# A routed feed-forward kernel: the transposes of the next pass's rows take their place on VectorE behind the last result issued before them

## The chip, the cores and the metric

The kernel runs on one core of one Trainium2 chip. The metric is the device time of one execution in microseconds (us), and the median over several executions. The engines are named as the profile names them: PE (matrix products; PEld is its loading of weights), DVE (VectorE), ACT (ScalarE), POOL (GpSimd) and SP (SyncE, which here issues loads). PE writes its results to PSUM, from which DVE and ACT read them.

## The reference

`x` is (8, 3584, 192), float32. What is computed, in short:

```python
w   = softmax(weight)                             # 8 heads x 7 taps
y   = causal 7-tap convolution of x along the sequence, one set of taps for each 24 channels
y   = y.reshape(28672, 192)                       # tokens
lg  = y @ w_gate + modality_bias[modality_id]     # 8 experts
e   = argmax(lg);  g = softmax(lg)[e]             # one expert and one gate for each token
out = g * (relu(y @ w1[e]) @ w2[e])               # 192 -> 1024 -> 192
```

## The kernel before

**Two halves that overlap.** The tokens are convolved and gated on PE and the other engines in 19 groups. Each finished row is written, with its gate and its number, to a table in DRAM called `routed_rows`, sorted by expert; POOL does this with indirect DMAs (L212). The second half reads that table back. It is cut into *slots*: a slot is a run of rows of one expert, of 1 to 4 *passes* of T = 256 rows each (`PASSES_OF_SLOT`). The first and the last slots are short; the last ones, planned for what is left of each expert, are one pass long. The first half is done long before the last slots, which then run alone.

**A pass.** Products of float32 values are made of a rounded high part and the rest: `sxh`, `sxl`, `sxs` for the rows (`sxs` holds both parts of the last 64 channels), `w1b` and `w2b` for the weights, `hh` and `hl` for the hidden layer. A pass has four steps of 256 hidden units. In a step `first` puts ten products for 128 x 512 values into a PSUM buffer `hps` (L700); ACT makes `hh` of it (relu and rounding, L703), DVE makes `hl` (the rest, L704). `second` multiplies `hh` and `hl` by `w2b` into two buffers `po` (L718, L722); it runs `LAG` = 2 steps behind `first`, so the last two seconds of a pass stand among the first steps of the next one. After the fourth `second` comes `put`, for each of the two `po`: ACT scales one half by the gate (`lowp`, L734), DVE adds the other (`o`, L736), and POOL writes the 128 rows of `o` to their places in the output (L737). There are two `hps` and two `po` buffers, so PE can begin the next pass's `po` only when `o` has been read out of the old one.

**Rows and weights for the next pass.** SP loads the rows of two passes at a time (a *lot*) as `near` (128 channels), `far` (64 channels) and `tags` (gate and row number), L650; there are three buffers of `near` and of `far`. `Slot.turn(k)` brings the rows of one pass into the shape that PE wants: DVE transposes in squares of 32 (`tp<-near` L676, `tp<-far` L678, two `tp` buffers), ACT rounds (`sxh`, `sxs`, L685), DVE subtracts (`sxl`, `sxs`, L687). The program issues the turn of the next pass in the second step (`fp == TURN`, L873) of the current one. Weights of the next slot are split by the same pair, ACT L100 and DVE L101, into eight parts spread over the steps of a slot: in a slot of one pass all eight fall into that pass, in a slot of four passes two into each. Groups of the first half also use L100 and L101, for `xh`/`xl` among others.

**Order.** ACT keeps the order in which the program is written (`ORDERED`, L898). The order on the other engines is chosen by a scheduler, which may move an instruction ahead of others when their data dependences allow it. `tc.issue_after(ins)` makes what is issued under it keep behind `ins` on its queue. `hl` and `o` are the DVE results of a pass; the two transposes depend only on the loads of `near` and `far` and on a free `tp`.

Of the kernel before, what the change touches and what calls it, by code (L numbers as in the profile page):

```python
# [14 lines left out]
ALU = mybir.AluOpType  # L15
# [17 lines left out]
T = 256  # L33
# [10 lines left out]
def conv_then_routed_ffn(ctx, tc, x, weight, modality, w_gate, mod_bias, w1, w2, out):  # L44
    nc = tc.nc
    NB, S, D = x.shape
# [9 lines left out]
    NJ = T // P  # L56
    OVER = 2
    Q = 32
# [25 lines left out]
    def ring(pool, n, shape, dtype, name, tag=None):  # L84

        tag = tag or name
        k = turns[tag] = turns.get(tag, -1) + 1
        return pool.tile(shape, dtype, name=name, tag=f"{tag}_{k % n}", bufs=1)

    def f(ap):  # L90
        return ap.bitcast(F32)
# [19 lines left out]
    def warm(n):  # L111
# [9 lines left out]
        out=tri, in_=ones, compare_op=ALU.is_gt, fill=0.0, base=0,  # L121
# [102 lines left out]
    class Group:  # L224
# [71 lines left out]
        def turn(self, q):  # L296

            t0 = 4 * q % NB
            self.turned = ring(gp, 2, [P, NK, 4, Q], F32, "turned")
            nc.vector.transpose(out=self.turned.rearrange("p k t c -> p t k c"),  # L300
                                in_=self.ys[4 * q // NB][:, t0:t0 + 4, OVER:W].rearrange("p t (k c) -> p t k c", c=Q))
# [32 lines left out]
        def choose(self):  # L334

            n = self.tiles
            lg = self.lg

            def per_tile(ap):
                return ap.unsqueeze(2).broadcast_to([MB, n, E])  # L340

            top = rt.tile([MB, NT], F32, name="top")[:, 0:n]
            nc.vector.tensor_reduce(out=top, in_=lg, axis=AX.X, op=ALU.max)
            ex = rt.tile([MB, NT, E], F32, name="ex", bufs=1)[:, 0:n]
            nc.vector.tensor_tensor(out=ex, in0=lg, in1=per_tile(top), op=ALU.subtract)
            nc.scalar.activation(out=ex, in_=ex, func=AF.Exp)
            self.oh = rt.tile([MB, NT, E], BF16, name="oh")[:, 0:n]
            rk = rt.tile([MB, NT, E], F32, name="rk", bufs=1)[:, 0:n]
            nc.vector.tensor_tensor(out=rk, in0=lg, in1=per_tile(top), op=ALU.is_equal)
            nc.vector.tensor_tensor(out=rk, in0=rk, in1=ramp.unsqueeze(1).broadcast_to([MB, n, E]), op=ALU.mult)  # L350
            first = rt.tile([MB, NT], F32, name="first")[:, 0:n]
            nc.vector.tensor_reduce(out=first, in_=rk, axis=AX.X, op=ALU.max)
            nc.vector.tensor_tensor(out=self.oh, in0=rk, in1=per_tile(first), op=ALU.is_equal)
            den = rt.tile([MB, NT], F32, name="den")[:, 0:n]
            nc.vector.tensor_reduce(out=den, in_=ex, axis=AX.X, op=ALU.add)
            nc.vector.tensor_scalar(out=den, in0=den, scalar1=1e-9, scalar2=None, op0=ALU.add)
            for i, y in enumerate(self.ys):
                nc.vector.reciprocal(out=y[0:MB, 0:self.nb, 0], in_=den[:, i * self.nb:(i + 1) * self.nb])
                with tc.issue_after(state["scatter"]) if "scatter" in state else nullcontext():
                    nc.gpsimd.iota(y.bitcast(I32)[0:MB, 0:self.nb, 1], pattern=[[S, self.nb]],  # L360
                                   base=self.b0 * S + (self.block + i) * MB + MB - 1,
                                   channel_multiplier=-1)
# [118 lines left out]
    state, tables = {}, {}  # L481
# [123 lines left out]
            routed(chunk, ins)  # L605


    class Slot:


# [62 lines left out]
        def turn(self, k):  # L673
            lot, k0 = divmod(k, LOT)
            tp = ring(sp, 2, [P, NJ + 1, P], F32, "tp")
            nc.vector.transpose(out=tp[:, 0:NJ].rearrange("p j (s t) -> p (j s) t", t=Q),  # L676
                                in_=self.rows[lot][:, k0 * T // Q:(k0 + 1) * T // Q])
            nc.vector.transpose(out=tp[:, NJ].rearrange("p (s t) -> p s t", t=Q), in_=self.ends[lot][:, k0])  # L678
            xh = ring(sp, 2, [P, NJ, P], F32R, "sxh")
            xl = ring(sp, 2, [P, NJ, P], F32R, "sxl")  # L680
            xs = ring(sp, 2, [P, NJ, P], F32R, "sxs")
            pieces = [(xh, xl, tp[:, 0:NJ, :])]
            pieces += [(xs[halves[j], j, :], xs[halves[1 - j], j, :], tp[halves[j], NJ, :]) for j in range(NJ)]
            for hi, _, raw in pieces:
                nc.scalar.copy(out=hi, in_=raw)  # L685
            for hi, lo, raw in pieces:
                turned = nc.vector.tensor_tensor(out=lo, in0=raw, in1=f(hi), op=ALU.subtract).ins  # L687
            self.h["x", k] = [z.rearrange("p j s -> p (j s)") for z in (xh, xl, xs)]
            self.h["tag", k] = self.tags[lot][:, k0 * NJ:(k0 + 1) * NJ]
            state["vector"] = turned  # L690

        def first(self, k, fp):
            wa = w1b[self.i % 2]
            mv = self.h["x", k]
            hps = ring(ps_g1, 2, [P, 2, T], F32, "hps")
            for u in range(2):
                fs = slice((2 * fp + u) * P, (2 * fp + u + 1) * P)
                terms = ((0, 0), (0, 1), (2, 0), (1, 2), (3, 2))
                for n, (c, z) in enumerate(terms):
                    nc.tensor.matmul(hps[:, u, :], wa[:, c, fs], mv[z], start=n == 0, stop=n == len(terms) - 1)  # L700
            hh = ring(hp, 3, [P, 2, T], F32R, "hh")
            hl = ring(hp, 3, [P, 2, T], F32R, "hl")
            nc.scalar.activation(out=hh, in_=hps, func=AF.Relu)  # L703
            nc.vector.scalar_tensor_tensor(out=hl, in0=hps, scalar=0.0, in1=f(hh), op0=ALU.max, op1=ALU.subtract)  # L704
            self.h[k, fp] = hh, hl

        def second(self, k, fp):
# [22 lines left out]
        def put(self, tag):  # L730
            for j, po in enumerate(self.po):
                gate = tag[:, j, 0:1]
                lowp = ring(sp, 2, [P, D], F32, "lowp")
                nc.scalar.activation(out=lowp, in_=po[:, D:2 * D], func=AF.Copy, scale=gate)  # L734
                o = ring(sp, OUTS, [P, D], F32, "o")
                nc.vector.scalar_tensor_tensor(out=o, in0=po[:, 0:D], scalar=gate, in1=lowp, op0=ALU.mult, op1=ALU.add)  # L736
                st = nc.gpsimd.indirect_dma_start(  # L737
                    out=out, out_offset=bass.IndirectOffsetOnAxis(ap=tag.bitcast(I32)[:, j, 1:2], axis=0),
                    in_=o, in_offset=None, bounds_check=N - 1, oob_is_err=False).ins
                tc.declare_no_dep(st, group="out", reason="each row is written once")  # L740
                tc.add_to_no_dep_group("out", st)
# [156 lines left out]
    with tc.manual_schedule(engines=ORDERED):  # L898
        run(0, always)
    state.pop("load")  # L900
    n_live = nc.values_load(state["n_live"][0:1, 0:1], min_val=0, max_val=plan[-1][1])
    with tc.If(n_live > always - plan[-1][0]):
        start(always)
# [26 lines left out]
```

## Time and profile before

| what | value |
|---|---|
| median of 3 runs | 1307.16 us (1306.64 to 1310.5) |
| profiled execution | 1303.86 us, its span 1302.1 us |
| PE busy | 1230.6 us (95%) |
| PEld busy | 1196.0 us (92%) |
| DVE busy | 1005.1 us (77%) |
| ACT busy | 725.3 us (56%) |
| POOL busy | 525.9 us (40%) |
| mean granted PE clock | 0.976 |
| HBM read / written | 118.16 / 51.82 MB |

The profiled execution is one of its own, beside the three timed ones. Times in a row count from the start of its span. A row of the timeline gives the start and the duration of one instruction, its engine, line, operation and tiles (output <- inputs), and in brackets how long the engine had waited and for what. A row of a window gives the busy time and the count of each engine in that stretch. `SPq` is the queue of DMA issues on SP. PE stands at nine tenths or more in all slices of the span but the first few and the last three.

### The profile page before, as it was taken

To read this page: it belongs to the slowest core of one execution; us is meant where nothing else is said; L and a number is where in the kernel's file an instruction comes from. 1 tells how busy PE (TensorE), PEld (TensorE's weight loads), DVE (VectorE), ACT (ScalarE), POOL (GpSimd) and SP (SyncE) were. 2 spreads that over 40 slices of the span, in tenths; PEclk is the share of its full clock that TensorE was granted. 3 is DMA by queue.
4 is the path that set the end of the run, shared out by engine and by line. 5 is a ranking of instruction groups with operands and counts; after the bars stand their busy time and mean duration, and the time that the engine had idled before them with its cause. 6 is when DMAs were issued, how large, how long until landed. Compare 5 with 4: busy or idle time off the path is not lost.

```text
span 1302.1 us, 28498 instructions
## 1 busy us (share of the span) xinstructions
PE 1230.6 (95%) x9106; PEld 1196.0 (92%) x9106; DVE 1005.1 (77%) x2545; ACT 725.3 (56%) x1644; POOL 525.9 (40%) x574
## 2 busy tenths in 40 slices
PE   8659998999999999999999999999999999999877
PEld 7438898999999999999999999999999999989877
DVE  6559986787888788887888788877886666677774
ACT  2226564556565656656665556565555555556663
POOL 5744763535353432625353532625344222221221
PEclk9769998999999999999999999999999999999998
DMA  6567474335444445423446345523533234883130
GB/s 176 156 182 155 142 177 89 94 82 138 101 113 98 103 94 118 130 58 98 86 117 150 98 90 122 135 53 92 103 82 90 43 96 97 177 198 100 28 92 16
DMA packets 314837, 142.24 MB, mean 109 GB/s; under 512 B 229043, under 2 KB 301356, under 8 KB 314677
## 3 DMA queue, kind: packets, MB, share of 16 engines
q1 hardware_dynamic: 289060, 94.97, 34.3%
q0 software_dynamic: 23232, 44.30, 10.8%
q8 instruction: 73, 1.20, 0.4%
q10 hardware_dynamic: 2384, 1.06, 0.3%
q14 instruction: 88, 0.71, 0.2%
HBM read 118.16 MB, written 51.82 MB: 131 GB/s over the span
## 4 chain that ended last, share of the span: by engine, by line
PE 73%; DVE 8%; DMA 7%; issue 4%; POOL 3%; SPq 3%; ACT 1%; DVEq 0%; POOLq 0%
PE hps L700 33%; PE po L718 22%; PE po L722 10%; PE cv L276 5%; PE gt L320 3%; POOL routed_rows L212 2%; DMA out_dram<-o,tags 2%; SPq L650 2%; DMA raw<-in_moe_w_dram 2%; DVE hl L704 1%; DVE w1b L101 1%; DMA near<-routed_rows 1%; DVE w2b L101 1%; DVE turned L300 1%; POOL out_dram L737 1%
## 5 line engine op out<-in xcount | busy, mean ns | idle before, releaser
L718 PE MATMUL po<-w2b,hh 128*128 128x384 f32 x1824 | 560.1, 357 | 22.8 <-DVE o L736 22.5
L703 ACT ACTIVATE hh<-hps 128x512 fp32r<-128x512 f32 x456 | 273.2, 599 | 409.9 <-PE hps L700 404.8
L700 PE MATMUL hps<-sxh,w1b 128*128 128x256 f32 x1824 | 486.6, 289 | 3.4 <-DVE hl L704 3.3
L737 POOL DMA_INDIRECT out_dram<-o,tags x228 | 240.1, 1053 | 575.7 <-DVE o L736 510.9
L722 PE MATMUL po<-w2b,hl 128*128 128x192 f32 x1824 | 443.8, 253 | 0.0
L704 DVE SCALAR_TENSOR_TENSOR hl<-hps,hh 128x512 fp32r<-128x512 f32 x456 | 310.9, 682 | 161.1 <-ACT hh L703 157.2
L718 PEld LDWEIGHTS po<-w2b,hh 128*128 128x128 f32 x1824 | 345.4, 189 | 27.5 <-DVE o L736 27.1
L700 PE MATMUL hps<-sxs,w1b 128*128 128x256 f32 x1824 | 365.6, 282 | 0.8 <-DVE sxs L687 0.8
L700 PEld LDWEIGHTS hps<-sxh,w1b 128*128 128x128 f32 x1824 | 346.4, 190 | 11.0 <-DVE hl L704 6.4
L722 PEld LDWEIGHTS po<-w2b,hl 128*128 128x128 f32 x1824 | 347.4, 191 | 0.0
L212 POOL DMA_INDIRECT routed_rows<-y,idx x256 | 253.7, 991 | 150.6 <-issue 102.5
L700 PEld LDWEIGHTS hps<-sxs,w1b 128*128 128x128 f32 x1824 | 281.8, 190 | 1.3 <-DVE sxs L687 1.0
L700 PE MATMUL hps<-sxl,w1b 128*128 128x256 f32 x912 | 257.2, 282 | 0.6 <-DVE sxl L687 0.6
L700 PEld LDWEIGHTS hps<-sxl,w1b 128*128 128x128 f32 x912 | 173.8, 191 | 3.0 <-DVE sxl L687 0.8
L101 DVE TENSOR_TENSOR w1b<-raw,w1b 128x512 fp32r<-128x512 f32 x152 | 102.4, 684 | 10.3 <-ACT w1b L100 8.7
L734 ACT ACTIVATE lowp<-po,tags 128x192 f32<-128x192 f32 x228 | 83.7, 418 | 32.2 <-PE po L718 31.7
L281 ACT COPY y<-cv 112x192 f32<-112x192 f32 (+1 forms) x198 | 53.7, 319 | 82.5 <-PE cv L276 58.0
L736 DVE SCALAR_TENSOR_TENSOR o<-po,tags,lowp 128x192 f32<-128x192 f32 x228 | 84.8, 410 | 16.3 <-DMA out_dram<-o,tags 13.1
L101 DVE TENSOR_TENSOR w2b<-raw,w2b 128x384 fp32r<-128x384 f32 x152 | 82.4, 552 | 15.1 <-ACT w2b L100 15.1
L100 ACT CAST w1b<-raw 128x512 fp32r<-128x512 f32 x152 | 92.3, 621 | 0.7
L100 ACT CAST w2b<-raw 128x384 fp32r<-128x384 f32 x152 | 76.0, 513 | 1.0
L687 DVE TENSOR_TENSOR sxs<-tp,sxs 64x128 fp32r<-64x128 f32 x228 | 66.3, 291 | 7.4 <-ACT sxs L685 0.4
(133 smaller groups left out, 1037.7 us busy)
## 6 DMA issues: line engine op xcount, KB each, us to landing
raw<-in_moe_w_dram SPq DMA_DIRECT2D x38, 768.0 KB
raw<-in_moe_w_dram SPq DMA_DIRECT2D x38, 512.0 KB
raw<-in_moe_w_dram SPq DMA_DIRECT2D x76, 256.0 KB
xr<-in_x_dram SPq DMA_DIRECT2D x36, 384.0 KB
near<-routed_rows SPq DMA_DIRECT2D x212, 64.0 KB
x<-in_x_dram SPq DMA_DIRECT2D x26, 384.0 KB
far<-routed_rows SPq DMA_DIRECT2D x456, 16.0 KB
routed_rows<-filler SPq DMA_DIRECT2D x8, 776.0 KB
```

The lines of the kernel that those rows point to most:

```text
L100: nc.scalar.copy(out=hi, in_=raw)
L101: return nc.vector.tensor_tensor(out=lo, in0=raw, in1=f(hi), op=ALU.subtract).ins
L212: state["scatter"] = nc.gpsimd.indirect_dma_start(out=scr, out_offset=bass.IndirectOffsetOnAxis(ap=idx, axis=0), in_=src, in_offset=None,).ins
L687: turned = nc.vector.tensor_tensor(out=lo, in0=raw, in1=f(hi), op=ALU.subtract).ins
L700: nc.tensor.matmul(hps[:, u, :], wa[:, c, fs], mv[z], start=n == 0, stop=n == len(terms) - 1)
L703: nc.scalar.activation(out=hh, in_=hps, func=AF.Relu)
L704: nc.vector.scalar_tensor_tensor(out=hl, in0=hps, scalar=0.0, in1=f(hh), op0=ALU.max, op1=ALU.subtract)
L718: nc.tensor.matmul(po, hh[:, u, js], wb[:, c, :], start=c == 0, stop=c == NF - 1, skip_group_check=True)
L722: nc.tensor.matmul(po[:, 0:D], hl[:, u, js], wb[:, c, 0:D], start=False, stop=False, skip_group_check=True)
L734: nc.scalar.activation(out=lowp, in_=po[:, D:2 * D], func=AF.Copy, scale=gate)
L736: nc.vector.scalar_tensor_tensor(out=o, in0=po[:, 0:D], scalar=gate, in1=lowp, op0=ALU.mult, op1=ALU.add)
L737: st = nc.gpsimd.indirect_dma_start(out=out, out_offset=bass.IndirectOffsetOnAxis(ap=tag.bitcast(I32)[:, j, 1:2], axis=0), in_=o, in_offse ...
```

## The change

A function `turn_behind` keeps the last instruction made by `hl` or `o`, and `turn` issues its two transposes behind the one that is kept. Nothing else is changed; lines behind it move by 3 to 4.

```diff
+    def turn_behind(op):
+        state["o"] = op.ins
...
         def turn(self, k):
             lot, k0 = divmod(k, LOT)
             tp = ring(sp, 2, [P, NJ + 1, P], F32, "tp")
-            nc.vector.transpose(out=tp[:, 0:NJ].rearrange("p j (s t) -> p (j s) t", t=Q),
-                                in_=self.rows[lot][:, k0 * T // Q:(k0 + 1) * T // Q])
-            nc.vector.transpose(out=tp[:, NJ].rearrange("p (s t) -> p s t", t=Q), in_=self.ends[lot][:, k0])
+            with tc.issue_after(state["o"]) if "o" in state else nullcontext():
+                nc.vector.transpose(out=tp[:, 0:NJ].rearrange("p j (s t) -> p (j s) t", t=Q),
+                                    in_=self.rows[lot][:, k0 * T // Q:(k0 + 1) * T // Q])
+                nc.vector.transpose(out=tp[:, NJ].rearrange("p (s t) -> p s t", t=Q), in_=self.ends[lot][:, k0])
...
-            nc.vector.scalar_tensor_tensor(out=hl, in0=hps, scalar=0.0, in1=f(hh), op0=ALU.max, op1=ALU.subtract)
+            turn_behind(nc.vector.scalar_tensor_tensor(out=hl, in0=hps, scalar=0.0, in1=f(hh), op0=ALU.max, op1=ALU.subtract))
...
-                nc.vector.scalar_tensor_tensor(out=o, in0=po[:, 0:D], scalar=gate, in1=lowp, op0=ALU.mult, op1=ALU.add)
+                turn_behind(nc.vector.scalar_tensor_tensor(out=o, in0=po[:, 0:D], scalar=gate, in1=lowp, op0=ALU.mult, op1=ALU.add))
...
     with tc.manual_schedule(engines=ORDERED):
         run(0, always)
     state.pop("load")
+    state.pop("o")
```

The queue of DVE, in the last slots of one pass each, before the change. `raw_1_86` and `raw_1_88` are the next slot's weights as loaded, `w1b_90` and `w2b_764` the places of their low parts; x2 is two of the same in a row.

```order
L704 SCALAR_TENSOR_TENSOR hl<-hps,hh 128x512
L676 STREAM_TRANSPOSE tp<-near 128x256
L736 SCALAR_TENSOR_TENSOR o<-po,tags,lowp 128x192 x2
L101 TENSOR_TENSOR w1b_90<-raw_1_86,w1b_90 128x512 x2
L687 TENSOR_TENSOR sxl<-tp,sxh 128x256
L687 TENSOR_TENSOR sxs<-tp,sxs 64x128 x2
L704 SCALAR_TENSOR_TENSOR hl<-hps,hh 128x512
L101 TENSOR_TENSOR w2b_764<-raw_1_88,w2b_764 128x2x192 x2
L678 STREAM_TRANSPOSE tp<-far 128x128
L704 SCALAR_TENSOR_TENSOR hl<-hps,hh 128x512
```

Here the transpose of `near` stands ahead of the two `o`, and it belongs to a later pass than the `sxl` and `sxs` behind them. The same place with the change:

```order
L708 SCALAR_TENSOR_TENSOR hl<-hps,hh 128x512
L740 SCALAR_TENSOR_TENSOR o<-po,tags,lowp 128x192 x2
L680 STREAM_TRANSPOSE tp<-near 128x256
L101 TENSOR_TENSOR w1b_90<-raw_1_86,w1b_90 128x512 x2
L682 STREAM_TRANSPOSE tp<-far 128x128
L691 TENSOR_TENSOR sxl<-tp,sxh 128x256
L691 TENSOR_TENSOR sxs<-tp,sxs 64x128 x2
L708 SCALAR_TENSOR_TENSOR hl<-hps,hh 128x512
L101 TENSOR_TENSOR w2b_764<-raw_1_88,w2b_764 128x2x192 x2
L708 SCALAR_TENSOR_TENSOR hl<-hps,hh 128x512
```

Both transposes now stand behind the two `o`, and those of a pass directly ahead of its own `sxl` and `sxs`, with two weight splits between them.

The queue of DVE in a pass in the middle of the run that also splits a part of `x` for the first half (the pass that runs from 786 us in the trace), before the change:

```order
L704 SCALAR_TENSOR_TENSOR hl<-hps,hh 128x512
L736 SCALAR_TENSOR_TENSOR o<-po,tags,lowp 128x192 x2
L101 TENSOR_TENSOR xl<-xr,xh 128x768
L101 TENSOR_TENSOR w1b_90<-raw_1_86,w1b_90 128x512
L687 TENSOR_TENSOR sxl<-tp,sxh 128x256
L687 TENSOR_TENSOR sxs<-tp,sxs 64x128 x2
L704 SCALAR_TENSOR_TENSOR hl<-hps,hh 128x512
L101 TENSOR_TENSOR xl<-xr,xh 128x768
L676 STREAM_TRANSPOSE tp<-near 128x256
L704 SCALAR_TENSOR_TENSOR hl<-hps,hh 128x512
```

The transposes of this pass's turn are not among these rows: they had been issued earlier, and the one in the ninth row belongs to the next turn. With the change:

```order
L708 SCALAR_TENSOR_TENSOR hl<-hps,hh 128x512
L740 SCALAR_TENSOR_TENSOR o<-po,tags,lowp 128x192 x2
L680 STREAM_TRANSPOSE tp<-near 128x256
L682 STREAM_TRANSPOSE tp<-far 128x128
L101 TENSOR_TENSOR xl<-xr,xh 128x768
L101 TENSOR_TENSOR w1b_90<-raw_1_86,w1b_90 128x512
L691 TENSOR_TENSOR sxl<-tp,sxh 128x256
L691 TENSOR_TENSOR sxs<-tp,sxs 64x128 x2
L708 SCALAR_TENSOR_TENSOR hl<-hps,hh 128x512
L101 TENSOR_TENSOR xl<-xr,xh 128x768
```

Both transposes now follow the two `o`, ahead of the splits of `x` and of the weights. On ACT and POOL the order is the same as before, on PE one pair of instructions is swapped, and on SP a few loads of `xr` (L254) stand among the loads of `near` at two places.

## The prediction

> **What bounds the kernel now.** I read the busy time by stage first. Each row gives a stretch, its length, then busy time and count for PE, PEld, DVE, ACT and POOL, and the granted PE clock.
>
> ```profile
> 990.00:1146.00 156.00, 156.00 (x1209) 156.00 (x1209) 106.76 (x255) 84.28 (x188) 33.69 (x34) 1.00 0.49 104
> 1146.00:1281.00 135.00, 119.31 (x871) 117.50 (x871) 101.86 (x227) 83.03 (x185) 27.34 (x24) 0.96 0.39 92
> ```
>
> Until 1146 us PE is never idle, so nothing that DVE does there can gain much. From 1146 us on PE stands still 15.7 of 135 us. To size that stretch I count passes: each pass issues two `lowp`, and these rows count them (DVE, then ACT), and then come the first matmuls of three passes.
>
> ```profile
> 988.30:1146.40 158.10, 12.62 (x34) 12.48 (x34) 1.00 0.49 104
> 1146.40:1280.70 134.30, 8.64 (x24) 8.80 (x24) 0.96 0.39 92
> ...
> 988.37 0.30 PE L700 MATMUL hps<-sxh,w1b 128*128 128x256 f32 x1
> 1146.49 0.31 PE L700 MATMUL hps<-sxh,w1b 128*128 128x256 f32 x1
> 1280.81 0.30 PE L700 MATMUL hps<-sxh,w1b 128*128 128x256 f32 x1
> ```
>
> So 17 passes took 158.12 us, 9.30 each, with PE full; the next 12 took 134.32 us where 12 × 9.30 is 111.6. These last passes cost 22.7 us more than PE needs. The waits of that stretch (1146 to 1281 us), in us, times and longest, say why:
>
> ```profile
> PE po L718 <- DVE o L736: 12.6, 6, 4.1
> PE hps L700 <- DVE hl L704: 3.1, 1, 3.1
> DVE tp L676 <- DMA near<-routed_rows: 16.1, 7, 4.3
> ```
>
> PE's 15.7 us fall together with DVE's 16.1 us. One of the six cases in order of time, DVE, ACT, PE and the SP queue:
>
> ```profile
> 1202.60 0.69 DVE L704 SCALAR_TENSOR_TENSOR hl<-hps,hh 128x512 fp32r<-128x512 f32 x1 [0.42 <-ACT hh L703]
> 1205.56 0.45 DVE L676 STREAM_TRANSPOSE tp<-near 128x256 f32<-128x256 f32 x1 [2.27 <-DMA near<-routed_rows]
> 1205.93 0.70 DVE L736 SCALAR_TENSOR_TENSOR o<-po,tags,lowp 128x192 f32<-128x192 f32 x2
> 1206.55 1.28 DVE L101 TENSOR_TENSOR w1b<-raw,w1b 128x512 fp32r<-128x512 f32 x2
> ...
> 1202.83 0.73 ACT L734 ACTIVATE lowp<-po,tags 128x192 f32<-128x192 f32 x2 [0.26 <-PE po L718]
> ...
> 1206.36 0.44 PE L718 MATMUL po<-w2b,hh 128*128 128x384 f32 x1 [2.12 <-DVE o L736]
> ...
> 1200.34 1.86 SPq L650 DMA_DIRECT2D near<-routed_rows  x4
> ```
>
> The inputs of `o` were ready when `lowp` ended at 1203.56, but `o` started only after the transpose ahead of it, which waited for rows asked for at 1200.34. `o` frees the PSUM bank that PE's next `po` needs, so PE stood 2.12 us for a transpose whose result nobody wanted for another pass.
>
> **The gain at the end.** With the change the transpose ahead of these `o` is gone; the one behind them reads rows that landed about a pass earlier. The row asked for at 1200.34 had landed by 1205.56. In the new order its reader comes after the next pass's `o`. A pass starts at 1198.26 (row below) and its `o` would end at 1203.29 + 0.74 = 1204.03, 5.8 us in; the next starts some 9.7 us later (worked out below), so its `o` end near 1213.7, 8 us after the landing. All 15.7 us of waits go. The remaining 7.0 of the 22.7 us are mostly PE at a low clock behind the gaps:
>
> ```profile
> 1162.00:1166.00 4.00, 4.00 (x21) 4.00 (x22) 2.04 (x4) 1.00 (x3) 0.00 (x0) 0.61 0.37 94
> 1230.00:1234.00 4.00, 4.00 (x21) 4.00 (x20) 3.70 (x9) 1.14 (x3) 1.65 (x2) 0.58 0.14 49
> 1266.00:1270.00 4.00, 3.58 (x18) 3.56 (x19) 3.90 (x11) 0.00 (x0) 2.46 (x2) 0.69 0.14 35
> ...
> 1228.96 0.44 PE L718 MATMUL po<-w2b,hh 128*128 128x384 f32 x1 [2.06 <-DVE o L736]
> ```
>
> At clocks of 0.61, 0.58 and 0.69 these stretches lose 0.39, 0.42 and 0.31 of 4 us, 4.5 us together, behind gaps of 3.1, 2.06 and 4.1 us. Without the gaps I let them go. The Trainium skill, "TensorE: Matmul & The Clock Gate", Part 1 on the clock gate, says that the array falls to half clock only after an idle window of about 3.4 us; by that the first two spells would not come from these gaps and 3.2 us would stay, and the sum below would be 3.2 us higher. The trace disagrees, with a spell right behind 2.06 us.
>
> **What the move costs at the end.** Moving behind `o` puts both transposes between `o` and the splits of the next pass's squares. ACT has a fixed order: `lowp`, weight casts, casts of `sxh` and `sxs` (which need the transposes), then `hh`; DVE's `hl` needs that `hh`, and the next pass's first matmul writes the PSUM buffer that this `hl` reads.
>
> ```profile
> 1210.37 0.30 DVE L678 STREAM_TRANSPOSE tp<-far 128x128 f32<-128x128 f32 x1
> ...
> 1204.79 0.62 ACT L685 CAST sxs<-tp 64x128 fp32r<-64x128 f32 x2
> 1205.43 0.60 ACT L703 ACTIVATE hh<-hps 128x512 fp32r<-128x512 f32 x1
> ...
> 1198.26 0.30 PE L700 MATMUL hps<-sxh,w1b 128*128 128x256 f32 x1
> ```
>
> In the new order (`hl`, `o` twice, near, `w1b` twice, far, splits), with those durations and 0.08 us of overlap between neighbours as in the rows: `o` end 1204.03; near 1203.95 to 1204.40; two `w1b` to 1205.60; far to 1205.82; ACT's two `sxs` casts wait for it, to 1206.5; `hh` to 1207.1; `hl` to 1207.8. Without any stall the next pass would start at 1198.26 + 9.30 = 1207.56. So it starts 0.3 to 0.45 us late; I take 0.4 for each of the seven passes with doubled weight splits: 2.8 us. The bounds are 0 (the far transpose hidden, as in a pass whose `hl` is in time) and 1.0 each (both transposes and a `w1b` split in full). Gain at the end: 22.7 − 2.8 = 19.9 us.
>
> **What it costs before 1146 us.** A plain pass, in which the transposes stood behind the third `hl`:
>
> ```profile
> 1012.00 0.74 DVE L736 SCALAR_TENSOR_TENSOR o<-po,tags,lowp 128x192 f32<-128x192 f32 x2
> 1012.72 0.57 DVE L101 TENSOR_TENSOR w2b<-raw,w2b 128x384 fp32r<-128x384 f32 x1
> 1014.33 0.69 DVE L704 SCALAR_TENSOR_TENSOR hl<-hps,hh 128x512 fp32r<-128x512 f32 x1
> 1014.94 0.44 DVE L676 STREAM_TRANSPOSE tp<-near 128x256 f32<-128x256 f32 x1
> 1015.30 0.27 DVE L678 STREAM_TRANSPOSE tp<-far 128x128 f32<-128x128 f32 x1
> ...
> 1012.88 0.62 ACT L685 CAST sxs<-tp 64x128 fp32r<-64x128 f32 x2
> 1013.53 0.60 ACT L703 ACTIVATE hh<-hps 128x512 fp32r<-128x512 f32 x1
> ...
> 1016.24 0.31 PE L700 MATMUL hps<-sxh,w1b 128*128 128x256 f32 x1
> ```
>
> `hl` ends 1015.02, 1.2 us before it is needed. After the change: near to 1013.1, `w2b` to 1013.6, far to 1013.8, `sxs` casts to 1014.4 (0.9 later), `hh` to 1015.05, `hl` to 1015.8. That uses 0.75 of the 1.2 us; nothing reaches PE. That room is the cover: were the chain 0.5 us longer than I make it, every further tenth would cost a tenth in each such pass. Passes that also split `x` or the gate's squares have no room left:
>
> ```profile
> 791.24 0.74 DVE L736 SCALAR_TENSOR_TENSOR o<-po,tags,lowp 128x192 f32<-128x192 f32 x2
> 792.27 0.96 DVE L101 TENSOR_TENSOR xl<-xr,xh 128x768 fp32r<-128x768 f32 x1 [0.29 <-ACT xh L100]
> 794.84 0.69 DVE L704 SCALAR_TENSOR_TENSOR hl<-hps,hh 128x512 fp32r<-128x512 f32 x1
> ...
> 795.58 0.38 PE L700 MATMUL hps<-sxh,w1b 128*128 128x256 f32 x1
> ...
> 928.81 0.69 DVE L704 SCALAR_TENSOR_TENSOR hl<-hps,hh 128x512 fp32r<-128x512 f32 x1
> 929.55 0.39 PE L700 MATMUL hps<-sxh,w1b 128*128 128x256 f32 x1
> ```
>
> Here the next pass starts 0.05 us after `hl` ends. The transposes (0.36 and 0.27 us from start to start) come ahead of `xl`, which idled 0.29 us anyway; near to 792.34 and far to 792.5 make `xl` some 0.2 us late, and `hl` and PE with it. Sixteen passes between 190 and 930 us end so, the last at 929.55: 16 × 0.2 = 3.2 us, between 0 (the idle time hides all) and 16 × 0.63 = 10 us (it hides nothing).
>
> The wait attached by the change names an instruction of DVE's own queue and adds no semaphore. The casts, splits and `hh` stay where they are on ACT. On SP a few loads of `xr` now stand among the `near` loads of a lot at two places, and would hold them until `xl` has read the buffer, some 8 us later than their turn. SP then waits far longer for DVE's slot table before its next weights, so this costs nothing; without that cover it would be one late weight load, about 6 us each.
>
> ```profile
> SPq L615 <- DVE of L562: 37.5, 2, 18.8
> ```
>
> **Sum.** The profiled execution took 1303.86 us (span 1302.1, 1.8 around it): 1303.86 − 19.9 + 3.2 = 1287.2. It was 3.3 us quicker than the median of the runs, 1307.16, and below the lowest of them, 1306.64. The same 16.7 us off the median give **1290.5 us**.
>
> **The rivals.** *The room is smaller than I make it.* In its favour: the plain pass keeps less than 0.5 us, and the chain crosses between DVE and ACT three times. Against: the rows show 0.03 us from `sxs` to `hh`. If some 90 passes each lost 0.1 us, the time would be 1290.5 + 9 = 1299.5. *Slower:* the same cover gone altogether. ACT's `hh` behind casts that wait for the transposes makes `hl` late at every pass start. It decides from the point where the chain is 0.7 us longer than computed, since 90 passes then lose 0.22 us each, the 19.9 us of the end; at 0.25 us over the forecast it would be 1290.5 + 22.5 = 1313. No idle time in DVE's rows of a plain pass speaks for that. *The rows are still late:* the transposes, now behind `o`, hold `hl` instead. With half of the 12.6 us left it would be 1297. Against it stand the 8 us of lead; for it, that SP asks for these rows only after weight splits which the change itself delays by tenths. *Nothing comes of it,* because the waits move to another instruction of the same queue: 1307. The new order of DVE speaks against that.
>
> **Numbers.** The forecast has 0.66, the smaller room 0.15, late rows 0.08, no effect 0.06, slower 0.05. About 0.3% (3.9 us) is what a measurement of this kernel can tell from none. Faster: 0.66 + 0.08 + 0.12 of the 0.15 = 0.86; the same 0.03 + 0.06 = 0.09; slower 0.05. The range: downwards the forecast without any cost at the end and before (1284.5), and a little for the jitter of the runs, 1283; upwards the smaller room, 1301.
>
> **What would show it.** Right: after 1146 us no `tp` waits for `near`, no `po` of PE waits for `o`, twelve passes take about 114.4 us instead of 134.3, and the clock stays at 1.00 there. Each end pass shows PE waiting 0.3 to 0.45 us for `hl`. Before 1146 us passes such as the one at 786 us take 0.2 us more, and plain ones stay at 9.30. Wrong: plain passes longer than 9.30, ACT's `sxs` waiting for `tp` by over 1.5 us, or `tp` waiting for `near` behind `o`.

## The result: 31.5 us faster, about twice what was forecast

| | before | with the change |
|---|---|---|
| median | 1306.9 us (1304.99 to 1310.5, 4 runs) | 1275.36 us (1274.14 to 1276.73, 4 runs) |
| profiled execution | 1303.86 us, span 1302.1 | 1274.14 us, span 1272.4 |

The ratio is 0.9756, with a 95% interval from 0.9732 to 0.9779. The forecast was 1290.5 us, with a range from 1283 to 1301: the direction was right, the size was not, and 1275.36 lies below the range.

The 29.7 us between the two profiled executions can be laid out by the starts of passes (the first `hps` product of each in the timelines). I number passes by when they start in the trace of before.

| stretch | before | with the change | difference |
|---|---|---|---|
| to the start of the pass at 190 us | 190.36 | 189.56 | -0.8 |
| from there to the pass at 1146 us | 956.13 | 946.46 | -9.7 |
| the next twelve passes | 134.32 | 114.59 | -19.7 |
| the rest of the span | 21.29 | 21.79 | +0.5 |

The prediction had -19.9 for the third row and +3.2 for the second. So the end went as forecast, and the middle, where a small loss was forecast, gained.

**The end.** The stretches before and in the last twelve passes of the changed kernel (length, then busy time and count of PE, PEld, DVE, ACT, POOL, the granted PE clock, DMA share, GB/s), and then the first products of the first of these passes and of the one after the last:

```profile
978.00:1136.00 158.00, 158.00 (x1225) 158.00 (x1225) 106.55 (x262) 88.26 (x190) 35.39 (x36) 1.00 0.50 105
1136.00:1251.00 115.00, 113.92 (x869) 112.10 (x868) 101.02 (x226) 83.25 (x184) 25.08 (x24) 1.00 0.46 106
...
1136.02 0.31 PE L704 MATMUL hps<-sxh,w1b 128*128 128x256 f32 x1
1250.61 0.39 PE L704 MATMUL hps<-sxh,w1b 128*128 128x256 f32 x1
```

PE now stands still 1.1 of 115 us where it stood 15.7 of 135, and the clock is 1.00 throughout where it was 0.96. The waits of that stretch (us, times, longest) no longer hold a `tp` that waits for `near`, nor a `po` that waits for `o`:

```profile
ACT sxs L689 <- DVE tp L682: 8.0, 12, 1.0
PEld hps L704 <- DVE hl L708: 2.7, 7, 0.6
PE hps L704 <- DVE hl L708: 0.3, 1, 0.3
```

One of the last passes (it starts at 1192.42), DVE and then ACT, to be held against the case shown in the prediction:

```profile
1197.56 0.74 DVE L740 SCALAR_TENSOR_TENSOR o<-po,tags,lowp 128x192 f32<-128x192 f32 x2
1198.22 0.43 DVE L680 STREAM_TRANSPOSE tp<-near 128x256 f32<-128x256 f32 x1
1198.58 1.25 DVE L101 TENSOR_TENSOR w1b<-raw,w1b 128x512 fp32r<-128x512 f32 x2
1199.75 0.30 DVE L682 STREAM_TRANSPOSE tp<-far 128x128 f32<-128x128 f32 x1
1201.36 0.69 DVE L708 SCALAR_TENSOR_TENSOR hl<-hps,hh 128x512 fp32r<-128x512 f32 x1 [0.33 <-ACT hh L707]
...
1200.09 0.62 ACT L689 CAST sxs<-tp 64x128 fp32r<-64x128 f32 x2 [0.91 <-DVE tp L682]
```

`o` runs at once, the near transpose behind it finds its rows there, and the far one behind the two weight splits makes ACT's `sxs` casts 0.91 us late, so that `hl` ends 9.63 us into the pass. The seven last passes take 9.68 us each.

**The middle.** The stretch that the prediction passed over, in the kernel before and then (nearly the same passes) in the changed one:

```profile
190.00:990.00 800.00, 791.07 (x6007) 783.30 (x6006) 648.88 (x1597) 468.39 (x1049) 349.53 (x375) 1.00 0.44 103
```

```profile
189.00:980.00 791.00, 789.12 (x6012) 781.98 (x6012) 647.48 (x1596) 476.20 (x1049) 343.66 (x373) 1.00 0.44 104
```

Before, PE stood still 8.9 us in these 800 us; now 1.9 in 791. DVE's waits over the whole span, before and then with the change, name what has gone:

```profile
DVE tp L676 <- DMA near<-routed_rows: 18.1, 8, 4.3
DVE o L736 <- DMA out_dram<-o,tags: 13.1, 8, 4.4
```

```profile
DVE o L740 <- DMA out_dram<-o,tags: 1.8, 3, 0.9
```

`o` has four buffers, and a new `o` has to wait until the store of the fourth last has read its own. Four passes carry the whole gain:

| pass that starts (before) at | before | with the change |
|---|---|---|
| 190 us | 18.06 | 10.98 |
| 325 us | 12.49 | 10.74 |
| 390 us | 12.26 | 10.74 |
| 682 us | 11.83 | 10.74 |

That is 11.4 us. Against it stand the losses that were forecast: of the sixteen passes that the prediction counted (they end right after an `hl`), three are the ones at 325, 390 and 682 us; the other thirteen became 0.05 to 0.25 us longer, 1.8 us in all.

The size of these stalls differs between executions with one and the same order. In the profiles of e1 and e6 below, which keep the old order there, the pass at 190 us takes 18.64 and 16.25 us, and the one at 682 us 11.30 and 10.76.

How a transpose comes to hold a store can be followed in the trace of before. Here are DVE, POOL, and at the end DVE and PE again; L374 to L387 is the placement, in which a group of the first half works out to which rows its tokens go (`idx`):

```profile
168.64 0.45 DVE L676 STREAM_TRANSPOSE tp<-near 128x256 f32<-128x256 f32 x1 [2.00 <-DMA near<-routed_rows]
169.01 0.24 DVE L374 COPY ad<-rp 112x120 f32<-112x120 f32 x1
171.98 0.17 DVE L387 CAST idx<-row 112x16 int32<-112x16 f32 x1
...
172.94 0.95 POOL L212 DMA_INDIRECT routed_rows<-y,idx  x1 [7.61 <-ACT y L281]
193.87 1.64 POOL L737 DMA_INDIRECT out_dram<-o,tags  x1 [0.15 <-DVE hl L704]
...
200.65 0.42 DVE L736 SCALAR_TENSOR_TENSOR o<-po,tags,lowp 128x192 f32<-128x192 f32 x1 [4.45 <-DMA out_dram<-o,tags]
...
201.12 0.69 PE L718 MATMUL po<-w2b,hh 128*128 128x384 f32 x1 [4.77 <-DVE o L736]
```

The same places with the change:

```profile
166.15 0.28 DVE L374 COPY ad<-rp 112x120 f32<-112x120 f32 x1
168.33 0.18 DVE L387 CAST idx<-row 112x16 int32<-112x16 f32 x1
...
169.31 0.95 POOL L212 DMA_INDIRECT routed_rows<-y,idx  x1 [4.38 <-issue]
189.82 1.03 POOL L741 DMA_INDIRECT out_dram<-o,tags  x1 [0.15 <-issue]
...
195.05 0.80 DVE L740 SCALAR_TENSOR_TENSOR o<-po,tags,lowp 128x192 f32<-128x192 f32 x2
```

The transpose of rows that are wanted two passes later waits 2.0 us, and the placement stands behind it on DVE, most of it behind the transpose of `far` as well. `idx` is 3.6 us later than it is with the change (3.2 us by the start of its pass). POOL's first scatter (L212) starts 0.8 us after it in both kernels; sixteen scatters take 21 us; only then come the stores of `o`. The store that starts at 193.87 has not landed when `o` wants its buffer. Before, `idx` ended 3.62 us after the start of its pass, and now 0.39; for the placements ahead of the other three stalls it ends 0.93, 0.53 and 0.52 us earlier than before, by the starts of passes.

### The profile page after: what moved, and what is told of

The parts are those of the page before. It is cut to its first block, busy times and chain, and to the rows that moved or that the text cites. A ratio compares the mean times of both kernels' runs of the same rounds, so it can differ in the third digit from the quotient of the medians.

```text
span 1272.4 us, 28546 instructions
## 1 busy us (share of the span) xinstructions
PE 1221.3 (96%) x9106; PEld 1187.7 (93%) x9106; DVE 1001.7 (79%) x2545; ACT 736.9 (58%) x1644; POOL 519.2 (41%) x574
## 4 chain that ended last, share of the span: by engine, by line
PE 77%; DVE 7%; issue 4%; DMA 4%; POOL 3%; SPq 2%; ACT 2%; DVEq 0%; POOLq 0%; ACTq 0%
PE hps L704 36%; PE po L722 23%; PE po L726 11%; PE cv L276 5%; PE gt L320 3%; POOL routed_rows L212 2%; DVE hl L708 2%; SPq L653 2%; DVE w1b L101 1%; DMA raw<-in_moe_w_dram 1%; DMA routed_rows<-y,idx 1%; DVE w2b L101 1%; DMA near<-routed_rows 1%; ACT lowp L738 0%; DVE sxs L691 0%
## 5 line engine op out<-in xcount | busy, mean ns | idle before, releaser
L741 POOL DMA_INDIRECT out_dram<-o,tags x228 | 233.6, 1024 | 555.8 <-DVE o L740 492.2
L704 PEld LDWEIGHTS hps<-sxh,w1b 128*128 128x128 f32 x1824 | 343.9, 189 | 12.7 <-DVE hl L708 7.9
L212 POOL DMA_INDIRECT routed_rows<-y,idx x256 | 253.7, 991 | 145.4 <-issue 114.2
L101 DVE TENSOR_TENSOR w2b<-raw,w2b 128x384 fp32r<-128x384 f32 x152 | 80.9, 542 | 10.3 <-ACT w2b L100 10.0
L689 ACT CAST sxs<-tp 64x128 fp32r<-64x128 f32 x228 | 67.9, 298 | 32.6 <-DVE tp L682 29.8
```

The costliest lines, as they stand in the source:

```text
L101: return nc.vector.tensor_tensor(out=lo, in0=raw, in1=f(hi), op=ALU.subtract).ins
L212: state["scatter"] = nc.gpsimd.indirect_dma_start(out=scr, out_offset=bass.IndirectOffsetOnAxis(ap=idx, axis=0), in_=src, in_offset=None,).ins
L741: st = nc.gpsimd.indirect_dma_start(out=out, out_offset=bass.IndirectOffsetOnAxis(ap=tag.bitcast(I32)[:, j, 1:2], axis=0), in_=o, in_offse ...
```

## The experiments

Each was timed against the kernel before on the same chip. The gain is worked out from the ratio and its interval and from the median of before in that call (1303 to 1304 us, 1306.9 for the change itself). The profile of each is cut in two as above: "early" from the second pass to the pass at 1146 us, "end" the next twelve passes. The start of the second pass moved between 99.5 and 104.9 us over all the profiles, whatever the kernel, so the stretches tell more than spans do. Chunk 8 holds the slots of two passes near the end, chunk 9 the last slots of one pass.

| run | gain in us (95%) | early | pass at 190 us | end |
|---|---|---|---|---|
| before | - | 1045.2 | 18.06 | 134.3 |
| the change | 31.9 (28.9 to 35.0) | 1036.3 | 10.98 | 114.6 |
| e1_end_only | 17.6 (15.4 to 19.7) | 1045.5 | 18.64 | 114.4 |
| e2_early_only | 10.3 (6.8 to 13.7) | 1036.8 | 11.30 | 133.7 |
| e3_one_turn | 2.7 (0.8 to 4.7) | 1042.3 | 15.72 | 133.0 |
| e4_before_o7 | 11.2 (9.0 to 13.4) | 1032.2 | 11.18 | 133.8 |
| e5_near_only | 21.1 (18.5 to 23.6) | 1041.7 | 15.79 | 117.4 |
| e6_rows_ready | 16.3 (13.2 to 19.3) | 1042.2 | 16.25 | 117.2 |
| e7_turn2 | -4.2 (-6.1 to -2.3) | 1060.1 | 11.99 | 121.3 |
| e8_after_o7 | 32.2 (29.6 to 34.8) | 1035.3 | 10.81 | 114.4 |
| e9_after_again | 29.1 (26.1 to 32.1) | 1037.3 | 11.35 | 114.6 |
| e10_two_slots | 7.0 (4.0 to 10.0) | 1038.5 | 11.01 | 134.9 |
| e11_far_free | 25.6 (22.3 to 28.7) | 1035.4 | 11.48 | 117.0 |
| e12_far_free_o7 | 28.8 (25.7 to 31.9) | 1033.3 | 10.80 | 114.2 |

### Two gains, or one

The condition at `turn` is narrowed to the end (e1) or to all but the end (e2):

```diff
-            with tc.issue_after(state["o"]) if "o" in state else nullcontext():
+            with tc.issue_after(state["o"]) if "o" in state and self.chunk >= 8 else nullcontext():
```

> Transposes go behind the last result only in the slots of two passes and of one pass at the end (chunks 8 and 9); everywhere else the scheduler places them as before. Theory (two separate gains): the twelve passes from about 1146 us take 114.6 us as in the changed kernel instead of 134.3, and the passes before stay as in the kernel before, the one of 18.06 us at 190 us among them: about 1287 us, 19 to 20 us under before. Rival (one gain, the earlier passes became quicker because of something that the end shares): over 1290 or under 1280 us.

```diff
-            with tc.issue_after(state["o"]) if "o" in state else nullcontext():
+            with tc.issue_after(state["o"]) if "o" in state and self.chunk < 8 else nullcontext():
```

> The converse: transposes behind the last result in chunks 0 to 7 only. Theory: the passes from 1146 us on keep their waits for rows (twelve passes 134 us), and the passes before take some 10.5 us less than before, mostly the one at 190 us (18.06 to 11.0) and those at 325, 390 and 682 us (1.1 to 1.75 each): about 1296 us. Rival (my prediction's term, a loss of 3.2 us there): 1310 us.

Each gives its own stretch and leaves the other as it was: 17.6 and 10.3 us, 27.9 together, where the whole change gave 31.9 and, timed again on another chip, 29.1 (e9). The rival of e2, the prediction's loss of 3.2 us, is out.

### Is it the ring of `o`

The kernel before with one number changed, and no order changed on any engine:

```diff
-OUTS = 4
+OUTS = 7
```

> The kernel before with 7 buffers of o instead of 4; the order on every engine is unchanged. Theory: o no longer waits for the stores behind POOL's scatters; the passes at 190, 325, 390 and 682 us lose their stalls (7.1, 1.75, 1.5 and 1.1 us): about 1295.5 us, and the end keeps its waits for near. Rival (those stalls come from the place of the transposes on DVE itself and not from the ring of o): 1307 us.

No `o` waits for a store any more, and the passes at 190, 325, 390 and 682 us take 11.18, 10.68, 10.74 and 10.74 us, while the end keeps its waits. So the stalls before 1146 us are waits for a buffer of `o`. More buffers take away even a little more of that stretch (13.0 us against 9.0): the pass at 978 us goes from 10.72 to 9.34, which the change leaves alone, and the thirteen passes above lose nothing.

> The changed kernel with 7 buffers of o instead of 4, no other order changed. Theory: the early order has already taken away nearly all waits of o for stores; what is left is the pass at 967 us (10.78 to 9.34, as with 7 buffers in the kernel before) and some tenths elsewhere: 1.5 to 3 us quicker than the changed kernel, 33 to 35 us under before. Rival (the two gains before 1146 us are independent): 40 us or more under before.

With both, the early stretch takes 1035.3 us: better than the change by 0.9 to 1.9 us, in the timed runs not to be told from it. The two remedies take away the same stalls, and do not add.

### What one transpose does

```diff
-            with tc.issue_after(state["o"]) if "o" in state else nullcontext():
+            with tc.issue_after(state["o"]) if self.i == 4 and k == 0 else nullcontext():
```

> Only one pair of transposes is put behind the last result: those of the rows of the ninth pass, of which the near one waited 2.0 us for its DMA at 168.6 us, ahead of the placement (L374 to L387) of a group. Theory: with that wait gone the placement ends 3.6 us earlier, POOL starts its 16 scatters as much earlier, the output stores behind them free the o buffers in time, and the pass at 190 us takes 11.0 us instead of 18.06: about 1300 us, 7 us less. Rival A (the 2.0 us wait costs what it lasts): 1305 us. Rival B (that pass's stall has nothing to do with this transpose): 1307 us.

At most a third of it came: 15.72 us instead of 18.06, not 11 (with the old order e6 has 16.25 there). The placement did move (`idx` 0.39 us into its pass, as with the whole change), and the scatters began 3.2 us earlier. POOL and DVE in that pass, which here starts at 190.55:

```profile
191.27 1.01 POOL L741 DMA_INDIRECT out_dram<-o,tags  x1 [0.15 <-issue]
192.59 1.16 POOL L741 DMA_INDIRECT out_dram<-o,tags  x1 [0.30 <-DVE hl L708]
...
196.71 0.42 DVE L740 SCALAR_TENSOR_TENSOR o<-po,tags,lowp 128x192 f32<-128x192 f32 x1 [0.25 <-DMA out_dram<-o,tags]
199.60 0.42 DVE L740 SCALAR_TENSOR_TENSOR o<-po,tags,lowp 128x192 f32<-128x192 f32 x1 [2.48 <-DMA out_dram<-o,tags]
```

The first store is nearly in time, 0.72 us into the pass (with the change 0.26). The second starts 2.04 us into it (1.60) and lands only 7.0 us later. So I asked whether the neighbouring turns bring the missing 0.45 us:

```diff
-            with tc.issue_after(state["o"]) if self.i == 4 and k == 0 else nullcontext():
+            with tc.issue_after(state["o"]) if self.i in (3, 4) else nullcontext():
```

> The transposes behind the last result in slots 3 and 4 only (the rows of passes 6 to 11), all others as before. With one pair alone the scatters began 3.2 us earlier but the pass at 190 us still took 15.7 us, since the second store was issued 2.04 us into it and landed behind the loads that follow. Theory (the transposes of the neighbouring passes bring the last 0.45 us): the second store is issued 1.6 us into the pass, lands before o wants its buffer, and the pass takes 11.0 us: 7 us under before. Rival (it is the run and not the order that decides such a close race): the pass takes 15 to 16 us again, 2 to 3 us under before.

They do. The pass starts at 192.51 here, its stores 0.26 and 1.60 us into it, and `o` runs without a wait that a row would show:

```profile
192.77 1.03 POOL L741 DMA_INDIRECT out_dram<-o,tags  x1 [0.15 <-issue]
194.11 0.98 POOL L741 DMA_INDIRECT out_dram<-o,tags  x1 [0.30 <-DVE turned L300]
...
197.90 0.93 DVE L740 SCALAR_TENSOR_TENSOR o<-po,tags,lowp 128x192 f32<-128x192 f32 x2
```

The pass takes 11.01 us, and the gain is 7.0 us; the passes at 325 and 390 us, whose turns are not moved, keep their stalls (14.0 and 12.5 us). The one at 682 us shows none (10.74), though its turn is not moved either. The rival of e10 is out. Rival A of e3 (a wait costs what it lasts) would have fitted the 2.7 us of e3; here the same 2.0 us of waiting, the only one that these two slots' transposes show, went with 7.0. And e3's own simple sum is out: whether a store lands in time is a close race, and between e3 and e10 four tenths of a us in its start went with 4.7 us of the pass.

### Is it the place, or the rows

The kernel before, with one operand changed at the end; the near transpose there reads zeros that are there from the start:

```diff
+    still = const.tile([P, T // Q, Q], F32, name="still")
+    nc.vector.memset(still, 0.0)
...
-                                in_=self.rows[lot][:, k0 * T // Q:(k0 + 1) * T // Q])
+                                in_=self.rows[lot][:, k0 * T // Q:(k0 + 1) * T // Q] if self.chunk < 8 else still)
```

> The kernel before, its transposes unmoved, but in the slots of chunks 8 and 9 the near transpose reads a constant tile that is there from the start instead of the near rows (the loads still run; the products of these slots are those of zeros in the first 128 channels). The transposes still stand ahead of o. Theory (the place alone costs nothing, the wait for the rows that it exposes does): no wait ahead of o, the end takes 9.3 us a pass, that is 22 us less than before and 2.6 us less than the changed kernel's end: about 22 us under before in all. Rival (a transpose ahead of o is itself what delays it, by its place): the seven passes stay above 10 us, gain under 8 us.

With nothing to wait for, the scheduler placed it some rows earlier than before, still ahead of `o`: between `far` and an `hl`. From 1192 to 1250 us PE hardly stands still:

```profile
1192.00:1250.00 58.00, 57.79 (x445) 57.44 (x445) 54.22 (x113) 45.88 (x104) 12.61 (x13) 1.00 0.36 81
...
1213.69 0.31 DVE L680 STREAM_TRANSPOSE tp<-far 128x128 f32<-128x128 f32 x1 [0.96 <-DMA far<-routed_rows]
1213.92 0.40 DVE L678 STREAM_TRANSPOSE tp<-still 128x256 f32<-128x256 f32 x1
```

Five of the seven last passes take 9.26 to 9.34 us, less than with the change. So a transpose ahead of `o` costs nothing as long as its rows are there; the rival (its place) is out, though the scheduler's own move means that the very same place was not tried. The end is 2.6 us longer than with the change, where 2.6 us less was expected, since now `far` transposes wait for their rows in front of a result, as at 1213.69. The waits of DVE over the whole span have four of them:

```profile
DVE tp L680 <- DMA far<-routed_rows: 7.2, 4, 3.3
```

Three passes of the end grow by 0.6, 1.9 and 2.7 us over what their like takes.

### What the two transposes cost apart

The changed kernel with only the near transpose behind the last result:

```diff
             with tc.issue_after(state["o"]) if "o" in state else nullcontext():
...
-                nc.vector.transpose(out=tp[:, NJ].rearrange("p (s t) -> p s t", t=Q), in_=self.ends[lot][:, k0])
+            nc.vector.transpose(out=tp[:, NJ].rearrange("p (s t) -> p s t", t=Q), in_=self.ends[lot][:, k0])
```

> The changed kernel, but only the transpose of near is put behind the last result; that of far goes where the scheduler likes, as before. Theory: near alone held o at the end, so the end keeps its gain; far is turned earlier, ACT's sxs casts no longer wait for it behind the weight splits, and the seven passes of the last slots take 9.3 to 9.5 us instead of 9.68: 0 to 2.5 us quicker than the changed kernel, 31 to 34 us under before. Rival (far, too, waits for its rows ahead of o): o waits again and the gain is under 25 us.

The term of the prediction holds: six of the seven last passes take 9.26 to 9.34 us here, so the 0.38 us of each came from the far transpose behind the weight splits. But the rival is right on the sum. A free `far` meets its rows too early:

```profile
1154.66 0.31 DVE L682 STREAM_TRANSPOSE tp<-far 128x128 f32<-128x128 f32 x1 [2.13 <-DMA far<-routed_rows]
```

An `hl` stands behind it, and that pass takes 12.81 instead of 9.27 us. The seventh of the last passes takes 11.32 us; `far` waits there as well. In the middle `idx` at the pass at 305 us ended 0.33 us into its pass (before 1.07, with the change 0.13), and the stalls at 190 and 325 us are back (15.79 and 12.39). I tried to have both, with `far` behind the last result only where it stood ahead of a placement or was seen to wait:

```diff
+            with tc.issue_after(state["o"]) if "o" in state and self.chunk in (0, 1, 2, 8) else nullcontext():
                 nc.vector.transpose(out=tp[:, NJ].rearrange("p (s t) -> p s t", t=Q), in_=self.ends[lot][:, k0])
```

The changed kernel again (e9), this version (e11), and this version with 7 buffers of `o` (e12):

> The changed kernel as it is, on the same chip as the next two, so that they can be compared with it: 30 to 32 us under before, with the pass at 190 us at 11.0 and the seven last passes at 9.68 us, as in its first profile.

> The changed kernel, but the transpose of far is put behind the last result only in chunks 0, 1, 2 and 8, where it would otherwise stand ahead of a placement or wait for its rows; elsewhere it is free, and near is behind everywhere. Theory: the seven last passes take 9.3 instead of 9.68 us (2.4 us) and the six passes of 0.13 us loss between 495 and 930 us lose nothing (0.8 us), with no stall back: 3 us quicker than the changed kernel. Rival (far ahead of a result brings a wait back somewhere): as quick as the changed kernel or slower.

> The same with 7 buffers of o: further 1.4 us from the pass at 967 us (10.78 to 9.34): 4.5 us quicker than the changed kernel, some 36 us under before. Rival (other stores come later in return, as nothing holds POOL's queue any more): no gain over the version with 4.

The rival holds again. With `far` free in chunk 9 two transposes of it wait, one of them for 3.65 us:

```profile
1165.27 0.31 DVE L683 STREAM_TRANSPOSE tp<-far 128x128 f32<-128x128 f32 x1 [3.65 <-DMA far<-routed_rows]
```

The seven last passes take 9.57 us on average instead of 9.68, and the end 117.0 us instead of 114.6. With 7 buffers of `o` as well the end came out at 114.2 and the early stretch at 1033.3 in the profile, and the timed runs cannot tell it from the change (28.8 and 29.1 us). Its order is that of e11 on every engine, yet its `far` transposes wait 3.6 us in all and those of e11 6.0, so a part of the difference is again a race. No version that I ran is clearly faster than the change.

### A later turn

```diff
-TURN = 1
+TURN = 2
```

> The changed kernel with TURN = 2: the turn of the next pass is issued in the third step of a pass, behind its third hl, instead of the second, behind o. Theory: the third hh no longer stands behind casts that wait for the transposes, so the 0.37 us in each of the seven last passes and the 0.13 us in some sixteen earlier ones go: 4 to 5 us quicker than the changed kernel, about 36 us under before. Rival (squares now come too late for the next pass's first product): PE waits for sxh, sxl or sxs at pass starts, and it is slower than the changed kernel, less than 31 us under before.

My theory fell: it is slower even than before. `hl` had room, but the squares had none. ACT, DVE and PE at the end of one of the last passes:

```profile
1231.71 0.41 ACT L689 CAST sxh<-tp 128x256 fp32r<-128x256 f32 x1 [1.42 <-DVE tp L680]
...
1231.24 0.44 DVE L680 STREAM_TRANSPOSE tp<-near 128x256 f32<-128x256 f32 x1
...
1232.17 0.39 PE L704 MATMUL hps<-sxh,w1b 128*128 128x256 f32 x1
1232.63 0.38 PE L704 MATMUL hps<-sxl,w1b 128*128 128x256 f32 x1
```

The near transpose now starts behind two weight splits; the first product of the next pass follows 0.05 us after the `sxh` cast, the second waits for `sxl`, and six of the seven last passes take 10.35 to 10.38 us instead of 9.68. The early stretch is 23.8 us longer than with the change; PE's waits for squares over the whole span make 12.7 us of rows. Shorter ones are not counted there, so where the rest of the 23.8 us goes is not shown:

```profile
PE hps L704 <- ACT sxh L689: 5.1, 10, 0.8
PE hps L704 <- DVE sxl L691: 5.0, 10, 1.5
PE hps L704 <- DVE sxs L691: 2.6, 6, 0.8
```

## Why the prediction was wrong, step by step

**What bounds the kernel now: the step that failed.** "Until 1146 us PE is never idle, so nothing that DVE does there can gain much" was read from a row that begins at 990 us. The row from 190 to 990 us, which the prediction leaves out, shows PE standing still for 8.9 us, and behind the longest of these gaps the clock was low as well:

```profile
200.00:204.00 4.00, 2.88 (x10) 2.59 (x11) 2.89 (x7) 0.00 (x0) 1.98 (x2) 0.50 0.47 100
```

The sentence above the change that PE stands at nine tenths in all slices but the first few and the last three hides it too: the seventh slice, from 195 to 228 us, stands at eight. The list of waits was cut to the end as well: over the whole span `near` is waited for eight times and not seven, and `o` waits eight times for a store. The eighth wait for `near` is the one at 168.64 us. Of the 13.1 us between the sum (1287.2) and the profiled execution (1274.14) 12.9 lie here: forecast +3.2, measured -9.7. The gain outside the end was put at nothing, and the waits of `o` for its stores, which cost most of it, are no term of the sum.

**What the late transpose holds.** At the end the prediction named what stood behind the waiting transpose: `o`. At 168.64 us another result stood behind it, the placement, and its reader is on another engine: POOL, which puts its scatters ahead of the stores of `o`. The prediction looked for the costs of the moved transposes at the next pass start and for no gain from their leaving the old place, though in each of the three other passes, too, it left the placement 0.5 to 0.9 us earlier. e2, e4 and e10 show this chain for the pass at 190 us. For the other three e4 shows its end, the ring of `o`; the link to the placement is not shown by a run. At 325 us the stores start earlier in their pass with the change, 0.73 us into it instead of 1.44. The passes at 390 and 682 us do not fit the chain: their stores start 1.4 us into the pass with and without the change, and land later before. The loads of `near` there begin 1.3 and 1.5 us ahead of the pass, with the change 5.1 us ahead; that the stores then meet them is argued, not shown. At 682 us the stall was missing in e6 and e10 too, with the old order, so that the change took it away may be luck.

**The gain at the end: right.** Forecast 22.7 - 2.8 = 19.9, measured 19.7; twelve passes forecast at 114.4 and measured at 114.6 us. All 15.7 us of waits went, and with them the 7.0 us that were put down mostly to the low clock: the clock is 1.00 from 1136 to 1251 us. The sum with 3.2 us of low clock left would have been 3.0 us off. e6 shows that it was the wait for rows and not the place.

**The cost at the end: right.** Forecast 0.3 to 0.45, taken as 0.4, for seven passes; measured 9.68 against 9.30, 0.38. In the order of the prediction, from the start of the pass: `sxs` casts ended at 8.24 by the sum and at 8.29 in the trace, `hh` at 8.84 and 8.91, `hl` at 9.54 and 9.63. e5 takes this cost away with `far` alone.

**The cost before 1146 us: right in its place, too large.** Sixteen passes at 0.2 us were forecast; thirteen of them lost 1.8 us in all, 0.13 us each, and the other three were stalled ones that gained. That the idle time ahead of `xl` hid more of the transposes than I let it would explain the size, but no run tests it. Plain passes stayed at 9.27 to 9.34 us, so their room of 1.2 us was enough: no smaller room, and none of the 90 passes that the slower rival needed.

**The other rivals.** The rows were not late behind `o`: no transpose of `near` or `far` waits for a DMA in the changed kernel by a row of its waits. The `xr` loads among the `near` loads left no stall: the passes there take what they took.

**From the profile to the median.** The forecast went by a difference, 16.7 us off the median. The profiled executions differ by 29.7 and the medians by 31.5 us, so this step added little.

**The range** reached down to the forecast without any cost. No case in it let the transposes gain anything outside the end, since no wait there was taken up.

## What to carry to other kernels

Before a stretch is called full, ask for the idle time of the bounding engine over all of it, and for the list of waits of the whole span: a wait that falls out of the window under study may be the same wait at another place. An instruction that waits on a queue for data wanted only later delays whatever result stands behind it, and where that result feeds another engine's queue the bill comes 30 us later under another name (here: a full ring of output buffers). Two cheap runs tell such a chain apart: more buffers where it ends, and the move of the one instruction where it begins.

## What the runs showed of the hardware

**The low clock does not follow from the length of a gap, but from where the gap falls.** In e5 PE stood still for 1.8 us, and the clock behind it was low for 3.4 us; the row of the wait, then three stretches that follow one another:

```profile
PE hps L704 <- DVE hl L708: 1.8, 1, 1.8
...
1152.97:1156.38 3.41, 1.66 (x13) 1.43 (x12) 1.72 (x4) 0.96 (x2) 0.00 (x0) 1.00 0.21 27
1156.39:1159.79 3.40, 3.40 (x16) 3.40 (x15) 1.73 (x4) 1.16 (x3) 0.00 (x0) 0.50 0.55 137
1159.81:1163.20 3.39, 3.39 (x29) 3.39 (x28) 3.14 (x9) 2.90 (x7) 2.06 (x2) 1.00 0.93 242
```

In e11 it stood still for 2.9 us, and the clock stayed at 1.00:

```profile
PE hps L705 <- DVE hl L709: 2.9, 1, 2.9
...
1161.38:1164.77 3.39, 1.95 (x15) 1.71 (x14) 0.24 (x1) 1.96 (x4) 0.97 (x1) 1.00 0.69 131
1164.79:1168.18 3.39, 1.97 (x15) 1.97 (x16) 2.42 (x5) 0.42 (x1) 0.00 (x0) 1.00 0.05 4
```

So a gap of 1.8 us cost a pass 3.5 us, and one of 2.9 us cost 3.05. The stretches are not cut at will. In all fourteen traces the clock changes only at whole steps of 3.413 us from one of its changes to another, and between two steps it is 0.50 or 1.00. In e5 one window between two steps holds the whole gap, 1.75 us idle of 3.41, and the next runs at 0.50; in e11 a step cuts the gap, and each window has about 1.4 us of it. I counted these windows in the fourteen traces from 100 us to the end of PE's work, those with the clock at 1.00: of those in which PE was idle for less than 1.6 us none is followed by a low one (49 had over 1.0 us), of 9 with 1.6 to 1.84 us five are, and of 20 with 1.85 us or more all are. The limit in these runs is about half a window. The prediction's reading, that such spells stand behind gaps of 2 to 4 us and go with them, held; that each gap brings one does not: the gap of 2.12 us that it shows at 1206.36 left 1.83 us in one window, and the clock stayed at 1.00. The Trainium skill, "TensorE: Matmul & The Clock Gate", Part 1, has a window of about 3.4 us that runs freely, and the traces agree with it; it asks for a whole idle window, and there the traces disagree.

**A store's time to land differs with what else is moving.** The second store of the pass at 190 us landed at most 4.3 us after its start when it started 1.60 us into the pass, and 7.0 us after when it started at 2.04 (e3). In e3 the mean share of the DMA engines was 1.09 from 196 to 200 us, and the next rows and weights were being loaded. The Trainium skill, "Trainium Kernel Development and Optimization", Key Constraints, says that DMAs issued from SP, ACT and POOL run on the same 16 engines and interleave; these two landings agree with that, but no run here moved those loads away to show it.
